# Query groups of 16 units in a ring of two, half-width projections of k and v, a transposed block by DMA, and loads moved to ScalarE

## The chip, the cores and the metric

The kernel runs on one core of one Trainium2 chip. The metric is the device time of one execution in microseconds (us). The kernel before has a median of 1043.0 us over three runs (1042.58 to 1043.64). In the text PE is TensorE (matmul), DVE VectorE, ACT ScalarE, POOL GpSimd and SP SyncE; the last three can also issue DMAs, each from a queue that it works through in order.

## The reference: two attention blocks, forward and backward

Two blocks get inputs of 2048 tokens and 448 features each, in bf16. Their outputs are concatenated, and the gradients of all eight inputs are computed for a given grad_out, so there are nine outputs.

```python
# A: linear attention, 16 heads of 28
phi = lambda t: jnp.where(t > 0, t + 1, jnp.exp(t)) + 1e-6
pq, pk = phi(q), phi(k)
kv  = jnp.einsum("bhsd,bhse->bhde", pk, v)
z   = jnp.einsum("bhsd->bhd", pk)
num = jnp.einsum("bhqd,bhde->bhqe", pq, kv)
den = jnp.einsum("bhqd,bhd->bhq", pq, z)[..., None] + 1e-6
a   = (num / den) @ wo
# B: softmax attention, 16 query heads of 28, one shared k and v head
q = x @ wq; k = x @ wk; v = x @ wv
p = softmax(einsum("bhqd,bkd->bhqk", q, k) * 28 ** -0.5)
b = einsum("bhqk,bkd->bhqd", p, v) @ wo
out   = concatenate([a, b], axis=-1)
grads = vjp(grad_out)          # of x, wqkv, wo of A; of x, wq, wk, wv, wo of B
```

## The kernel before

The kernel has four stages. Only in the third is the order of instructions written out by hand (tc.manual_schedule, line 922). In the others a planner orders the work of each engine by its estimate of when things are ready; semaphores are set by the framework.

**Phase A** (lines 124 to 546, up to about 178 us of the profile) is the whole of block A, forward and backward, in 16 tiles of 128 tokens, and the preparation of B's weights. Per-head matrices of 28x28 are kept as block-diagonal 448x448 matrices in four chunks of 128 rows: kv_blk, kvT_blk and, in the backward pass, dkvT_blk (which takes the place of kvT_blk) and dkv_blk (which lies in R4). `blkprod` (line 289) makes such a matrix by full matmuls and masks the result on DVE. dkvT_blk comes from line 450 and dkv_blk, its transpose, from line 477; dkv_blk is used at line 484. In between lie `gw` (line 430: a weight gradient, evacuated by ACT and DVE at lines 442 to 446) and the loop of line 458. All DMA transposes of phase A are issued by SP. Lines 499 to 522 prepare B's weights: wq_pad (the query weights with each head padded from 28 to 32 columns, the first of which stays free), rep (the k and v weights, each repeated four times side by side, so that a projection leaves four copies of k in the four 32-partition strips), bsel (0/1 columns that add up the squares of each head) and wo_pr (wo in 16 loads, one per head). Behind the last tile, SP transposes B's part of grad_out into R2 (line 545).

**Phase B's preparation** (lines 548 to 621) projects x. For each of four chunks of 512 tokens and for k and v there are four matmuls of 128x128x512 that accumulate; ACT (k, line 583) and DVE (v, line 580) evacuate them straight into kT_rep and vT_rep. `k_max` (line 567) finds the largest squared norm of k. Then for each chunk the queries are projected in four groups g of four heads (line 603), evacuated by ACT into R1, squared by DVE, and four matmuls with bsel add the norms up into one PSUM tile (line 609). `q_shift` (line 623) turns norms and the largest k norm into a bound on the scores, on 16 partitions; `put_shift` (line 630) writes it by DMAs into the free rows of R1, so that the score matmul subtracts it. At the end 32 narrow matmuls (line 618) turn k and v back into token rows.

**The core** (lines 647 to 1049) is the attention itself. A block b stands for 256 query tokens (qc) and two heads (a pair; g = pair // 2 is the group of four heads), and has eight units, each a step over 256 key tokens; there are 64 blocks, 512 units, and 28 more to drain the pipeline. In unit u PE makes the scores of unit u and the dP of unit w = u - 16 (`rows_SD`); ACT makes two exponentials (lines 955, 997) and one copy, cp (line 971); DVE and POOL multiply dP by the exponentials into dsT, a half each (lines 967, 972); two units later DVE transposes dsT in blocks of 32 into dsx (line 1041). Every fourth unit SP issues a DMA transpose of four units of exponentials (eN<-eT, line 999), which the dv matmuls read. Between them lie small operations once a block, among them `o_copy`, `o_norm` and `row_D`, and projections of the output in parts.

The gradient of k (`dk_m`, line 865) needs the queries transposed, in qX. For that POOL copies a group's queries of one qc, four times side by side, into a staging tile, qst, with one buffer (`qc_copy`, two copies), and SP transposes that (`qc_T`, line 860). qX holds all four groups of a qc and has two buffers, one per pool. The set for qc 0 is made ahead of unit 0, by POOL and DVE in dsT buffers; the set for the next qc in units 29, 30, 37, 38, 45, 46, 53 and 54 of the 64 that a qc takes (lines 973 to 979, 1001). So four blocks running have copies, and four have none. Block b's dk matmuls run in the odd units from 8b + 27 on.

**The end** (post_load, line 761, and lines 1051 to 1129): from unit 512 on, SP loads grad_out and x again in four and four pieces, the first of them for the gradient of wo (`gwo`); then come the remaining weight gradients and the gradient of x.

Of the kernel before, what the change touches and what calls it, by code (L numbers as in the profile page):

```python
# [9 lines left out]
ALU = mybir.AluOpType  # L10
# [15 lines left out]
def kernel(  # L26
# [49 lines left out]
    kmax2 = cst.tile([H, 1], F32, name="kmax2")  # L76
    eps = cst.tile([H, 1], F32, name="eps")
# [46 lines left out]
    def phase_A(pa, cA, cB, awk, psA):  # L124
# [95 lines left out]
        zero = [t[:, c, :] for t in (kvT_blk, kv_blk, dkv_blk) for c in range(4)]  # L220
# [49 lines left out]
        for st in range(NS):  # L270
            if st + 2 < NS:
                xT(st + 2)
            kproj(st)
            if st >= 4:
# [176 lines left out]
        prod_to(VW, wvT, dkvT_blk, True)  # L451
        with tc.issue_after(gw(gqn, 0).ins):
# [47 lines left out]
        rep = K1[1].rearrange("p c h k -> p (c h k)")[:, 0:1024].rearrange("p (w c k) -> p w c k", w=2, k=P)  # L500
        nc.gpsimd.memset(rep, 0.0)
        nc.gpsimd.memset(wq_pad, 0.0)
        for w in range(2):
            for j in range(4):
                nc.gpsimd.tensor_copy(out=rep[:, w, 0:3, 32 * j + 1:32 * j + 1 + DH], in_=wkv[:, w, 0:3, :])
                nc.gpsimd.tensor_copy(out=rep[64:128, w, 3, 32 * j + 1:32 * j + 1 + DH], in_=wkv[64:128, w, 3, :])
# [4 lines left out]
        bsel = ga[:, 4, :].rearrange("p (g k) -> p g k", k=P)  # L511
        nc.gpsimd.memset(bsel, 0.0)
        for g in range(4):
            for j in range(4):
                nc.gpsimd.memset(bsel[32 * j:32 * j + 32, g, 4 * g + j:4 * g + j + 1], 1.0)
# [5 lines left out]
        wt = flat(ga[:, 5:7, :]).rearrange("p (a k) -> p a k", k=P)  # L521
        nc.sync.dma_start_transpose(wt, rep.rearrange("p w c k -> p (w c k)"))
# [17 lines left out]
        with tc.issue_after(o1.ins):  # L540
            for w in range(2):
                nc.gpsimd.dma_start(wkvT_d[32 * w:32 * w + 32, 0:3 * P], wt[0:32, 4 * w:4 * w + 3, :])
                nc.gpsimd.dma_start(wkvT_d[32 * w:32 * w + 32, 3 * P:D], wt[0:32, 4 * w + 3, 64:128])
        for q4 in range(4):
            dma_T(v4(R2), xa, 4 * q4, 4)
        return xbT, wq_pad, rep, bsel, ga[:, 8:12, :], [flat(gaB[:, 2 * i + 8:2 * i + 10, :]).bitcast(F32) for i in range(3)]

    def phase_B_pre(pa, cA, awk, psA, io):
        xbT, wq_pad, rep, bsel, sh, tmp = io
        kT, vT, vaug, kn, qT = kT_rep, vT_rep, vaug_, kn_, R1  # L550
# [4 lines left out]
        ones16 = cA.tile([P, H], BF16, name="ones16")  # L555
        nc.gpsimd.memset(ones16[:], 1.0)
        nc.gpsimd.memset(ones16[0:1, :], 0.0)
        neg = cA.tile([P, 1], F32, name="neg")
        nc.gpsimd.memset(neg[:], 0.0)
        for j in range(4):  # L560
            nc.gpsimd.memset(neg[32 * j:32 * j + 1, :], -1.0)
        sel = cA.tile([P, 32], BF16, name="sel")
        nc.gpsimd.tensor_copy(out=sel[:], in_=identB[:, 0:32])
        nc.gpsimd.memset(sel[0:1, :], 0.0)
        kmx = cA.tile([H, NQC], F32, name="kmx")
        sqk = []
        def k_max(qc, sq):
            ps = gen([H, 512])
            mm(ps[:, :], ones16[0:32, :], sq[0:32, :])
            nc.vector.tensor_reduce(out=kmx[:, qc:qc + 1], in_=ps[:, :], axis=AX.X, op=ALU.max)  # L570

        prev = None
        for qc in range(NQC):
            for w, dst in [(0, kT), (1, vT)]:
                ps = gen([P, 512])
                for c in range(4):
                    mm(ps[:, :], rep[:, w, c, :], xbT[:, c, qc * 512:(qc + 1) * 512], start=(c == 0), stop=(c == 3))

                if w:
                    nc.vector.tensor_scalar(out=dst[:, qc * 512:(qc + 1) * 512], in0=ps[:, :], scalar1=neg[:, 0:1],  # L580
                                            scalar2=None, op0=ALU.add)
                else:
                    nc.scalar.activation(out=dst[:, qc * 512:(qc + 1) * 512], in_=ps[:, :], func=ACT.Identity,
                                         bias=neg[:, 0:1])
            sq = awk.tile([P, 512], BF16, name="osb")
            nc.vector.tensor_tensor(out=sq[0:32, :], in0=kT[0:32, qc * 512:(qc + 1) * 512],  # L586
                                    in1=kT[0:32, qc * 512:(qc + 1) * 512], op=ALU.mult)
            if prev is not None:
                k_max(qc - 1, prev)
            prev = sq  # L590
        shifts = [flat(sh)[0:H, i * 512:(i + 1) * 512] for i in range(2)] + [flat(R3)[r:r + H, 5120:5632] for r in (32, 0)]
        for qc in range(NQC):
            qs = slice(qc * 512, (qc + 1) * 512)
            pn = psA.tile([P, 512], F32, name="aacc")
# [565 lines left out]
```

## Time and profile before

| what | us |
|---|---|
| median of three runs | 1043.0 |
| the profiled execution | 1044.09 |
| its span, first to last instruction | 1042.4 |
| phase A | 0 to 178.5 |
| phase B's preparation | 178.5 to 206.5 |
| core, start (first 27 units) | 206.5 to 245.7 |
| core, in full run | 245.7 to about 970 |
| drain and end | 970 to 1042 |
| busy in the span: PE / DVE / ACT / POOL | 1003.5 / 886.9 / 865.2 / 812.3 |

Busy time is the time in which an engine had at least one compute instruction running. Matmuls overlap in PE's pipeline, so the time that one costs is read from the distance between starts, not from its own length. A row of a timeline has the start, the length, the engine, the line, the operation, the result and its inputs, the shape, the count and, in brackets, how long the engine had been idle before and which work the profile takes to have released it. Rows of "SPq" are the instants in which SP works on a DMA issue. A line can be that of a helper: most full matmuls have line 81, most tiled ones line 676.

### The profile page before, as it was taken

How to read it: one execution, taken by the hardware profiler on the slowest of the kernel's cores; microseconds unless marked ns; L12 is line 12 of the kernel's file. 1: busy time of each engine (PE TensorE's matmuls, PEld its weight loads, DVE VectorE, ACT ScalarE, POOL GpSimd, SP SyncE). 2: the span in 40 equal slices, each digit the busy share in tenths (PEclk: the TensorE clock that was granted, in tenths of full speed). 3: DMA queues.
4: the chain of work that ended last, by engine and by line, in shares of the span. 5: the costliest groups of instructions: out<-in, count | busy, mean ns of one | idle time of the engine just before them, and what ended most of it. 6: DMA issues, size and time to landing. Idle time of an engine off the chain costs nothing.

```text
span 1042.4 us, 40109 instructions
## 1 busy us (share of the span) xinstructions
PE 1003.5 (96%) x16245; PEld 485.1 (47%) x16245; DVE 886.9 (85%) x1780; ACT 865.2 (83%) x1743; POOL 812.3 (78%) x1106
## 2 busy tenths in 40 slices
PE   9999999999999999999999999999999999999998
PEld 5555554434444444444444444444444444444444
DVE  7897500669999999999999999999999999999942
ACT  6463132599999999999999999999999999999632
POOL 8601282238998998999999989998999999889860
PEclk9999999999999999999999999999999999999999
DMA  9879999299999999999999999999999999999983
GB/s 261 157 137 191 176 229 218 38 161 201 194 187 192 187 193 194 202 187 194 201 193 195 192 187 204 198 182 202 188 197 186 195 195 195 200 188 203 228 168 90
DMA packets 689058, 195.15 MB, mean 187 GB/s; under 512 B 670408, under 2 KB 686688, under 8 KB 688872
## 3 DMA queue, kind: packets, MB, share of 16 engines
q1 hardware_dynamic: 680392, 179.97, 105.0%
q0 software_dynamic: 4544, 9.46, 3.0%
q10 hardware_dynamic: 3936, 3.16, 1.0%
q8 instruction: 127, 2.08, 0.8%
q14 instruction: 59, 0.48, 0.2%
HBM read 12.60 MB, written 10.84 MB: 22 GB/s over the span
## 4 chain that ended last, share of the span: by engine, by line
PE 39%; DVE 25%; POOL 16%; ACT 8%; issue 7%; DMA 3%; DVEq 0%; SPq 0%; ACTq 0%; POOLq 0%
PE agen L81 13%; POOL dsT L972 12%; DVE dsT L967 10%; PE agen L676 9%; DVE dsx L1041 9%; PE aacc L676 8%; PE aacc L81 7%; ACT cp L971 4%; ACT eT L997 2%; DMA eN<-eT 2%; DVE doT L852 1%; DVE R L986 1%; POOL qst L856 1%; POOL prod L821 1%; PE aacc L809 1%
## 5 line engine op out<-in xcount | busy, mean ns | idle before, releaser
L972 POOL TENSOR_TENSOR dsT<-cp,eT 128x512 bf16<-128x512 bf16 x512 | 584.6, 1156 | 49.4 <-ACT cp L971 42.6
L1041 DVE STREAM_TRANSPOSE dsx<-dsT 128x512 f32<-128x512 f32 x512 | 356.7, 697 | 5.8 <-POOL dsT L972 3.2
L676 PEld LDWEIGHTS <-R 32*128 32x128 bf16 (+1 forms) x9104 | 245.1, 94 | 243.3 <-issue 192.5
L967 DVE TENSOR_TENSOR dsT<-agen,eT 128x512 bf16<-128x512 f32 x512 | 340.3, 665 | 11.3 <-PE agen L676 5.4
L971 ACT ACTIVATE cp<-agen 128x512 bf16<-128x512 f32 x512 | 327.0, 639 | 11.8 <-PE agen L676 9.7
L955 ACT ACTIVATE eT<-aacc 128x512 bf16<-128x512 f32 x512 | 325.5, 636 | 12.0 <-PE agen L676 6.8
L997 ACT ACTIVATE eT<-aacc 128x512 bf16<-128x512 f32 x512 | 333.4, 651 | 0.0
L676 PE MATMUL agen<-dsx,qX 32*32 32x512 bf16 x4024 | 264.0, 376 | 0.0
L676 PE MATMUL agen<-doT,R 32*128 32x256 bf16 x2048 | 243.5, 269 | 4.1 <-DVE dsT L967 3.2
L676 PE MATMUL aacc<-R,R 32*128 32x256 bf16 (+1 forms) x2240 | 207.9, 267 | 16.7 <-DVE doT L852 6.6
L676 PE MATMUL agen<-dsT,R 128*32 128x256 bf16 x2048 | 155.5, 273 | 0.5 <-issue 0.5
L676 PE MATMUL agen<-eT,R 128*32 128x256 bf16 x2048 | 155.5, 273 | 0.1
L676 PEld LDWEIGHTS <-qX 32*32 32x32 bf16 x4096 | 78.3, 89 | 112.5 <-issue 54.1
L676 PE MATMUL aacc<-eN,don 128*32 128x512 bf16 x1024 | 91.7, 387 | 1.0 <-DMA eN<-eT 1.0
L81 PEld LDWEIGHTS <-R 128*128 128x128 bf16 x517 | 40.9, 98 | 41.0 <-issue 10.6
L81 PE MATMUL agen<-R,R 128*128 128x448 bf16 (+1 forms) x180 | 42.1, 361 | 0.3 <-DVE pq L244 0.3
L676 PEld LDWEIGHTS <-don 128*32 128x32 bf16 x1024 | 21.1, 93 | 42.5 <-issue 42.5
L856 POOL COPY qst<-R 128x512 bf16<-128x512 bf16 x56 | 34.2, 611 | 5.0 <-DVE dsx L1041 2.5
L821 POOL TENSOR_TENSOR prod<-R,oTs 128x128 f32<-128x128 bf16 x64 | 27.5, 430 | 9.0 <-DVE oTs L817 9.0
L586 DVE TENSOR_TENSOR osb<-R 32x512 bf16<-32x512 bf16 x4 | 1.7, 413 | 35.4 <-DMA R<-xa 33.8
L427 POOL COPY pk<-R 128x256 bf16<-128x256 bf16 x4 | 1.6, 399 | 37.7 <-DVE R L389 37.7
L262 POOL TENSOR_SCALAR wdq<-wdq 128x448 bf16<-128x448 bf16 x16 | 21.1, 1326 | 12.0 <-DVE phiT L243 12.0
(235 smaller groups left out, 1000.1 us busy)
## 6 DMA issues: line engine op xcount, KB each, us to landing
eN<-eT SPq DMA_TRANSPOSE x128
xa<-in_A_x_dram SPq DMA_DIRECT2D x8, 224.0 KB
ga<-in_grad_out_dram SPq DMA_DIRECT2D x4, 448.0 KB
out_dram<-osb ACTq DMA_DIRECT2D x16, 112.0 KB
xa<-in_grad_out_dram POOLq DMA_DIRECT2D x4, 448.0 KB, 7.1
out_dram<-wdq POOLq DMA_DIRECT2D x8, 224.0 KB, 5.5
eT<-in_grad_out_dram SPq DMA_DIRECT2D x4, 448.0 KB
eT<-in_B_x_dram SPq DMA_DIRECT2D x4, 448.0 KB
```

The lines of the kernel that those rows point to most:

```text
L81: nc.tensor.matmul(out_ap, lhsT=lhsT, rhs=rhs, start=start, stop=stop, tile_position=(0, 0))
L262: nc.gpsimd.tensor_scalar(out=wq_n[:, st, 0:D], in0=wq_n[:, st, 0:D], scalar1=1.0, scalar2=None, op0=ALU.min)
L676: nc.tensor.matmul(out, lhsT=lhsT, rhs=rhs, start=start, stop=stop, tile_position=pos, skip_group_check=True)
L809: nc.tensor.transpose(onp[:, qb, :, :].rearrange("p h c -> p (h c)"), oTs[0:64, qb * P:(qb + 1) * P], identF[0:64, 0:64], tile_position=(0 ...
L821: nc.gpsimd.tensor_tensor(out=prod[b][:], in0=dnv, in1=os_, op=ALU.mult)
L856: eng.tensor_copy(out=st.rearrange("p (b s) a j -> p b s a j", s=2)[:, :, s, :, :], in_=src.unsqueeze(2).to_broadcast([P, 4, 4, 32]))
L955: nc.scalar.activation(out=eT(u)[:, 0, :], in_=sp[0][:, :], func=ACT.Exp, scale=scale)
L967: nc.vector.tensor_tensor(out=dst[:, 0, :], in0=dp[0][:, :], in1=ew[:, 0, :], op=ALU.mult)
L971: nc.scalar.activation(out=cp[:, :], in_=dp[1][:, :], func=ACT.Copy)
L972: nc.gpsimd.tensor_tensor(out=dst[:, 1, :], in0=cp[:, :], in1=ew[:, 1, :], op=ALU.mult)
L997: nc.scalar.activation(out=eT(u)[:, 1, :], in_=sp[1][:, :], func=ACT.Exp, scale=scale)
L1041: nc.vector.transpose(out=dsx[b][:, tp, :, :, :].rearrange("p h t c -> p (h t c)").bitcast(F32), in_=dsT[y][:, :, :].rearrange("p h c -> p ...
```

## The change

- **dkv_blk** is no longer computed; four DMA transposes from dkvT_blk, issued by ScalarE right behind line 451, fill it, and POOL clears 64 rows. Four zero fills of it by ACT (line 275) go.
- **wo_pr** is loaded by four DMAs in place of 16. rep holds the weights once (32 columns of k and 32 of v), bsel has 32 columns, and their copies, fills, transposes and stores shrink with them.
- **Projection of k and v**: two PSUM tiles in place of eight, each with two chunks of tokens one above the other (64 partitions each); the two halves are matmuls with 64 columns of weights, issued in turn into the two halves of PE's columns. Four DMAs by POOL and four by SP replicate k and v into the strips of kT_rep and vT_rep. k_max, the token rows and the squares work on 64-partition halves, and the first two of these stand between the second and third query group of chunk 0.
- **Norms**: four matmuls into the four 32-column strips of PE, one per group, behind the first query group of the next chunk (the last ones at the end); q_shift works on 128 partitions.
- **Core**: qX has one group (qc, g), G = 4 qc + g, and a ring of two buffers from one pool. Group G is copied by POOL in units 16G + 13 and 16G + 14 and transposed by SP in unit 16G + 14, G = 0 too; nothing is made ahead of unit 0. Pools of 12 KiB a partition less follow from it, and later pools move up. row_D of block 0, which was skipped, runs in unit 12.
- **Behind the core** the four loads of grad_out are issued by ScalarE.

```diff
+        for c in range(4):
+            r = DC_ROWS[c]
+            nc.scalar.dma_start_transpose(dkv_blk[:, :, c * P:c * P + r], blks[0:r, (12 + c) * D:(12 + c) * D + 512])
+        nc.gpsimd.memset(dkv_blk[64:128, 3, :], 0.0)
...
-        for h in range(H):
-            g, j = divmod(h, 4)
-            nc.sync.dma_start(wo_pr[32 * j + 1:32 * j + 1 + DH, g, 0:D], B_wo[h * DH:(h + 1) * DH, :])
+        for j in range(4):
+            nc.sync.dma_start(wo_pr[32 * j + 1:32 * j + 1 + DH, :, 0:D],
+                              B_wo.rearrange("(g j r) d -> j r g d", j=4, r=DH)[j, :, :, :])
...
-        blkprod(dkv_blk, [lambda c, i: cols(GT[0], c, i), lambda c, i: cols(GT[1], c, i)], [lambda c: woT[:, c, :]])
...
+        for p in range(2):
+            ps = gen([P, 512])
+            for c in range(4):
+                for a in range(2):
+                    i_ = nc.tensor.matmul(ps[64 * a:64 * a + 64, :], lhsT=rep[:, c, 0:64],
+                                          rhs=xbT[:, c, (2 * p + a) * 512:(2 * p + a + 1) * 512], start=(c == 0),
+                                          stop=(c == 3), tile_position=(0, 64 * a), skip_group_check=True)
...
+        for w, dst in [(0, kT_rep), (1, vT_rep)]:
+            for a in range(2):
+                for j in range(4):
+                    [nc.gpsimd, nc.sync][w].dma_start(
+                        dst[32 * j:32 * j + 32, :].rearrange("r (p a s) -> r p a s", p=2, a=2)[:, :, a, :],
+                        kvs[64 * a + 32 * w:64 * a + 32 * w + 32, :, :])
...
+        def norms(qc):
+            pn = psA.tile([P, 512], F32, name="aacc")
+            for g in range(4):
+                i_ = nc.tensor.matmul(pn[32 * g:32 * g + 32, :], lhsT=bsel[:, 0:32], rhs=sqs[:, 4 * (qc % 2) + g, :], start=True,
+                                      stop=True, tile_position=(0, 32 * g), skip_group_check=True)
...
+                if qc == 0 and g == 1:
+                    k_max(0)
+                    k_max(1)
+                    kv_nat(0)
+                    kv_nat(1)
+                if qc and g == 0:
+                    pn = norms(qc - 1)
...
-                nc.sync.dma_start(t[:, :, 0:D], go2[rows, D:2 * D].rearrange("(t p) d -> p t d", p=P))
+                nc.scalar.dma_start(t[:, :, 0:D], go2[rows, D:2 * D].rearrange("(t p) d -> p t d", p=P))
...
+        def qc_T(G):
+            qX[G] = pq_.tile([P, 4, 2, P], BF16, name="qX")
+            nc.sync.dma_start_transpose(qX[G].rearrange("p b s c -> p (b s) c"), qst.rearrange("p n a j -> p (n a j)"))
...
-                if 0 <= gq < 4 and u < 448:
-                    if gq == 0 and iq == 0:
-                        qX[qq] = (pqb_ if qq % 2 else pqa_).tile([P, 4, 2, 512], BF16, name="qX")
-                    if iq < 2:
-                        qc_copy(nc.gpsimd, qst, qq, gq, iq)
+                if u == 12:
+                    row_D(0)
+                if hasS and u % 16 in (13, 14):
+                    qc_copy(u // 16, u % 16 - 13)
...
-                    if 0 <= gq < 4 and iq == 1 and u < 448:
-                        qc_T(qst, qq, gq)
+                    if u % 16 == 14:
+                        qc_T(u // 16)
```

More of the change, by code (lines that the diff above doesn't have):

```diff
@@ L219, in phase_A @@
             nc.gpsimd.memset(t[64:128, 3, :], 0.0)
-        zero = [t[:, c, :] for t in (kvT_blk, kv_blk, dkv_blk) for c in range(4)]
+        zero = [t[:, c, :] for t in (kvT_blk, kv_blk) for c in range(4)]
         wvT = w_T(wvT_, w3, 2 * D)
@@ L563, in phase_B_pre @@
[L563 to L572, printed above, removed]
+            nc.gpsimd.memset(sel[32 * j:32 * j + 1, :], 0.0)
+        kmx = cA.tile([P, NQC], F32, name="kmx")
@@ L573, in phase_B_pre @@
         for qc in range(NQC):
-            for w, dst in [(0, kT), (1, vT)]:
+            qs = slice(qc * 512, (qc + 1) * 512)
+            for g in range(4):
                 ps = gen([P, 512])
                 for c in range(4):
[L577 to L584, printed above, removed]
@@ L615, in phase_B_pre @@
[L615 to L619 removed]
+                    mm(ps[:, :], wq_pad[:, c, g * P:(g + 1) * P], xbT[:, c, qs], start=(c == 0), stop=(c == 3))
+                nc.scalar.activation(out=qT[:, g, qs], in_=ps[:, :], func=ACT.Copy)
+                nc.vector.tensor_tensor(out=sqs[:, 4 * (qc % 2) + g, :], in0=qT[:, g, qs], in1=qT[:, g, qs], op=ALU.mult)
```

149 lines of the change are left out of this document (67 added, 82 removed).

## Prediction

> **What bounds the kernel now.** The profile's stretches come first, because the change touches several stages with different limits.
>
> ```profile
> 178.50:206.50 28.00, 27.71 (x150) 11.83 (x147) 16.02 (x36) 14.43 (x24) 7.25 (x13) 1.00 0.33 61
> 206.50:245.70 39.20, 35.21 (x399) 14.47 (x395) 28.78 (x55) 34.79 (x68) 19.54 (x28) 1.00 0.97 167
> 245.70:970.00 724.30, 701.07 (x13860) 332.18 (x13860) 705.73 (x1389) 717.32 (x1454) 674.36 (x858) 1.00 1.21 194
> 970.00:1042.00 72.00, 64.86 (x694) 30.56 (x694) 36.16 (x66) 25.01 (x48) 36.62 (x52) 1.00 0.74 159
> ```
>
> Columns: length, then busy time of PE, weight loads, DVE, ACT and POOL, granted clock (1.00 throughout), DMA share, GB/s. From 178.5 to 206.5 (B's projections) PE is busy 27.7 of 28.0 us and every other engine at most 16: work taken from PE there shortens the stage. In the core (245.7 to 970) ACT is busy 99%, DVE 97%, PE 97%, POOL 93%.
>
> Next, the core in blocks of eight units, cut at DVE's evacuation of line 986 (once a block). Most blocks last 11.78 us (the last nine 12.08); a few are longer, such as the fourth and fifth of these:
>
> ```profile
> 434.96 0.43 DVE L986 TENSOR_SCALAR R<-agen 64x256 bf16<-64x256 f32 x1
> 446.74 0.43 DVE L986 TENSOR_SCALAR R<-agen 64x256 bf16<-64x256 f32 x1
> 458.52 0.43 DVE L986 TENSOR_SCALAR R<-agen 64x256 bf16<-64x256 f32 x1
> 470.76 0.43 DVE L986 TENSOR_SCALAR R<-agen 64x256 bf16<-64x256 f32 x1
> 483.81 0.43 DVE L986 TENSOR_SCALAR R<-agen 64x256 bf16<-64x256 f32 x1
> ```
>
> The last two steps are 12.24 and 13.05 us. Over blocks 12 to 52 the excess over 11.78 adds up to 7.8 us. Most of it stands at the end of the bursts in which four blocks running copy queries for the transpose (blocks 19, 20, 34, 35, 40, 48, 51). POOL's and SP's timelines say why:
>
> ```profile
> 464.57 0.61 POOL L856 COPY qst<-R 128x512 bf16<-128x512 bf16 x1 [0.46 <-DMA qX<-qst]
> 477.62 0.61 POOL L856 COPY qst<-R 128x512 bf16<-128x512 bf16 x1 [1.32 <-DVE dsx L1041]
> ...
> 460.19 1.30 SPq L860 DMA_TRANSPOSE qX<-qst  x1
> 461.60 11.66 SPq L999 DMA_TRANSPOSE eN<-eT  x2
> 473.35 1.26 SPq L860 DMA_TRANSPOSE qX<-qst  x1
> 474.72 10.65 SPq L999 DMA_TRANSPOSE eN<-eT  x2
> ```
>
> The staging tile qst has one buffer. Its transpose waits behind the big ones in SP's queue, about 6 us after the copies (454.0 to 460.2; 467.4 to 473.4), and POOL is released 4.3 us after the issue (460.19 to 464.57, 473.35 to 477.62; I read the second release as this DMA too, since the DVE work named has no part in qst). So the next block's first copy, due 11.78 - 1.66 (the step between the two copies) = 10.1 us after this block's second, comes too early. SP itself is over its time in such a block: 10.7 + 1.3 + gaps = 12.1 us against 11.78.
>
> **The change part by part.**
>
> (1) *Core: one query group per 16 units.* A staging reuse now has 23.56 - 1.66 = 21.9 us where it needs 10.4: these waits go. SP's demand in 16 units is 4 x 5.4 + 1.4 = 23.0 of 23.56 us, POOL's about 11.7 (with copies: 459.07 to 471.25 between two operations of line 821, less the wait of 0.46) + 10.6 (the same less two copies at 0.57) + 0.65 for a store = 22.9. What remains of the 7.8 us is about 0.3 at each of three output transposes (line 1048), and about 0.9 of the stalls around 805 to 818 us, where PE waited for eN: 6.0 us go (bounds 2.5 and 7.5). Eight more copies (64 for 56, 0.61 us each) fall mostly where none were; the last groups lie in blocks of 12.08 us, where POOL needs the same 22.9 of 24.2. The ring: group G is filled from unit 16G+14 on, its buffer was last read at 16G+9, and it is first read at 16G+27. Ready after 6 + 4.3 us, or 7 units: 6 units to spare.
>
> (2) *B's projections, PE.* Start to start from its timeline:
>
> ```profile
> 182.09 0.38 PE L81 MATMUL agen<-osb,ones 32*16 32x512 bf16 x1
> 182.41 1.90 PE L81 MATMUL agen<-pk,K 128*128 128x512 bf16 x8
> 184.24 0.38 PE L81 MATMUL agen<-osb,ones 32*16 32x512 bf16 x1
> ...
> 110.65 1.70 PE L85 MATMUL aacc<-R,xa 128*64 128x448 bf16 x16
> ...
> 429.76 0.40 PE L676 MATMUL aacc<-eN,don 128*32 128x512 bf16 x4
> ```
>
> Removed: 32 k/v matmuls at 1.83/8 = 0.229, 7.3; four k_max at 0.32, 1.3; 16 norm matmuls at 0.22, 3.5; 32 narrow ones at 0.033 (27 in 0.88), 1.05: together 13.1 us. Added: 16 half-width matmuls. The line 85 row has such pairs, two halves of the columns side by side: 16 start within 1.63 us at 448 columns, so 0.116 at 512, 1.9 us. Norms in four column strips: four of 512 columns take 0.40 alone and eight 0.62, so 0.3 a chunk, 1.2 us. k_max with half the rows: 0.7 (0.5 if pairs overlap, 1.3 if not). 16 matmuls of 64 columns: 0.7 (0.5 to 1.0). Two waits are new. At the end nothing lies between the last query projection and its norms (before, the narrow matmuls did): ACT 0.60, DVE 0.43 and handovers, 1.2 us. And DVE gets four maxima (0.61) and four copies (about 0.35), 3.9 us, in one place, against 3.1 us of PE work that needs no buffer from it: 0.7 (0 to 1.5). Added 6.4, gain 6.7 us. If no pairs overlapped, k/v would cost 3.7 and norms 3.5, and the gain fall to 2.6; at best it is 8.5. ACT loses three evacuations of 0.69 and DVE three of 0.73; both have room.
>
> The Trainium skill's TensorEngine Tiling (Array Packing), Restrictions, says that column tiling goes without fast weight loading. By that alone a pair might cost what two full matmuls do, and the sum would be that of rival D; the line 85 row, where 16 of them keep their 0.10 us pace with their loads, disagrees for this shape.
>
> (3) *dkv_blk by transpose.* 32 matmuls (126.29 to 128.14) go, 1.85 us on a PE without idle time there. Added are four issues on ScalarE. SP's like ones take 1.4 each (two in 2.79); on ScalarE that is 5.6 us. If they go out when dkvT_blk is masked (about 102), they end before its next work at 110.4 and land long before 126. Gain 1.85; nothing below that in the good case, the bad one is rival B.
>
> (4) *Replication of k and v by eight DMAs.* POOL's four issues (0.55 each) follow its last at 182.3, and land near 188; the first unit would start near 197. SP's four follow the transposes that end at 185.5; v is first used at unit 16. Hidden; each us later than 197 would cost one.
>
> (5) *Fewer loads, copies and fills in set-up* (wo_pr, rep, bsel, wkvT_d): POOL's chain there ends at 146.4 and only stores and a load follow that is needed at 171; SP has the slack. Nothing. Four zero fills less on ACT, which waits for PE there: nothing.
>
> (6) *Start of the core.* Four POOL and four DVE copies and four SP transposes go; PE runs without a gap there but for 0.70 at 207.7, where it waits for ACT. I take 0.4 (0 to 0.7). The added row_D of block 0 (DVE 0.28, POOL 0.4) falls into 6.8 us of POOL idleness.
>
> (7) *Loads behind the core by ScalarE.* PE waits 0.16 us for the first at 982.6, so little is to be won. ScalarE's issue at unit 516 must wait for POOL's product of unit 515, and behind it stands ScalarE's cp, for which POOL and PE wait; cp already waits for POOL there (1.32 and 0.80 us at 977.9 and 979.2). Cost between -0.2 and 1.3; I take 0, the nearer end.
>
> Sum: 6.0 + 6.7 + 1.85 + 0.4 = 15.0 us. The profiled execution took 1044.1 (span 1042.4 and 1.7 around it), so 1029.1 by its time; it lay 1.1 above the median, 1043.0. Forecast **1028.0**, its own range 1024 to 1032.
>
> **Rivals.**
>
> *B: ScalarE's transposes queue behind SP's.* SP has transposes at 105.0 to 111.6 and on to 117.7; ScalarE is in order, and its evacuations at 110.4 and 112.4 stand behind. If it starts after 111.6 + 4.3 and issues 5.6 us, the one at 112.4 is 9 us late; DVE's next products wait for that, and PE has four buffers of 0.76 = 3 us of cover: 6 lost. If the planner lets the evacuations by and the transposes wait for 117.7, dkv_blk lands at 117.7 + 4.3 + 5.6 + 4.3 = 132 for a use at 126: the same 6. Both at once reach 12. Time 1034 (1031 to 1040). For it: SP's queue is full there. Against: the rows show idle ScalarE from 103.5 to 110.4. Chance 0.14. The Trainium skill's DMA: Bandwidth & Descriptors, section Silent corruption: two transposing streams in flight at once, demands just this wait of the later stream. By it this rival is the rule; no run here shows it, since all transposes before go out from SP.
>
> *C: the core keeps its stalls*, since line 999 and 1048 alone make them; gain 9: 1034. For: the stall at 805 us. Against: the releases of qst above. 0.10.
>
> *D: pairs don't overlap* on these shapes, so the change doesn't do what it should: 4.1 less, 1032. 0.06.
>
> *E, slower: the query groups come late.* Before, a whole set had over 30 units of lead; now 6. If SP ran more than 19 - 4.3 = 14.8 us behind (it runs 5 to 6.5 behind), PE would wait for each group; at the longest stall seen, 1.3 us, 32 groups cost 41: 1069. At 0.5 us a group it would be level. 0.08.
>
> **How the numbers follow.** Forecast 0.62. B, C and D end at 1032 to 1034. All that is faster: 0.88. Within 0.2% (2.1 us, about what a measurement of this kernel can tell from no change): B's worst together with C, or E at its threshold, 0.04. Slower: 0.08. The range 1024 to 1036 holds the forecast, most of B, C and D, and the bounds of the waits.
>
> **What would show it.** Right: the stage of B's projections 20 to 22 us long, 16 half-width matmuls starting within 2 us; blocks of 11.8 us throughout, no POOL wait ahead of qst; no matmuls for dkv_blk. Wrong: idle PE in the stages of lines 458 or 484, DVE or ACT waiting there for ScalarE's queue; PE waits for qX in the core; a gap longer than 2 us ahead of unit 0.

## The result and the profile after

The changed kernel takes 1049.7 us (median of four runs, 1049.1 to 1051.8); the kernel before took 1042.9 beside it (1042.6 to 1043.6). The ratio is 1.007, with a 95% interval of 1.005 to 1.0091: it is **slower by 6.8 us** where the forecast was 15 us faster. The profiled execution has a span of 1047.7 us (before 1042.4). The stages of that execution, with the columns of the prediction's first view (the second number is PE's busy time, the one ahead of the last two the granted clock):

```profile
178.50:189.00 10.50, 10.50 (x58) 5.29 (x58) 0.00 (x0) 2.72 (x5) 1.45 (x2) 1.00 1.02 212
189.00:209.80 20.80, 20.66 (x119) 8.04 (x121) 14.12 (x34) 13.09 (x21) 11.37 (x22) 1.00 0.80 117
209.80:249.00 39.20, 34.25 (x384) 14.34 (x389) 25.50 (x51) 34.91 (x68) 17.43 (x25) 1.00 0.86 160
249.00:970.10 721.10, 700.57 (x13860) 332.50 (x13860) 704.85 (x1388) 715.94 (x1454) 677.65 (x862) 1.00 1.20 194
970.10:1047.70 77.60, 67.09 (x694) 30.75 (x694) 36.30 (x66) 25.04 (x48) 37.60 (x54) 0.96 0.80 164
```

B's projections start at 189.0 instead of 178.5 and take 20.8 us instead of 28.0. The core is cut again at DVE's evacuation once a block (line 986, now 995); b0 is its first row, b61 the 62nd. The ledger of the two executions:

| stage | before | after | difference | forecast |
|---|---|---|---|---|
| phase A, to the start of B's projections | 178.5 | 189.0 | +10.5 | -1.85 |
| B's projections | 28.0 | 20.8 | -7.2 | -6.7 |
| start of the core, to b0 | 39.2 | 39.2 | 0 | -0.4 |
| b0 to b53 | 632.8 | 627.3 | -5.5 | -6.0, with the next |
| b53 to b61 | 96.9 | 99.2 | +2.3 | |
| b61 to the end | 67.0 | 72.2 | +5.2 | 0 |

**Phase A.** Three engines' timelines of the changed kernel, ACT, SP and PE in this order:

```profile
97.84 1.83 ACT L249 ACTIVATE gaT<-aacc 128x448 bf16<-128x448 f32 x4 [0.42 <-PE aacc L81]
111.46 10.76 ACTq L454 DMA_TRANSPOSE R<-blks  x4
122.26 0.95 ACT L326 CAST KOT<-agen 128x448 bf16<-128x448 f32 x2 [22.59 <-DMA R<-blks]
...
105.58 10.31 SPq L419 DMA_TRANSPOSE ga<-gaT  x2
123.48 2.48 SPq L109 DMA_TRANSPOSE ga<-R  x2
...
122.84 14.02 PE L81 MATMUL agen<-KOT,R 128*128 128x448 bf16 x62 [9.96 <-ACT KOT L326]
```

ACT's first transpose goes out only at 111.46, and its four take until 122.22, because SP's take turns with them: SP too stands still for ScalarE's to land, twice (its waits: total us, times, longest):

```profile
SPq L109 <- DMA R<-blks: 7.4, 1, 7.4
SPq L419 <- DMA R<-blks: 4.7, 1, 4.7
```

The evacuation of line 326 stands behind them in ACT's queue, and PE idles 9.96 us for it. PE's clock falls meanwhile (the last but two column):

```profile
110.00:115.00 5.00, 2.89 (x23) 1.23 (x21) 0.00 (x0) 0.00 (x0) 0.00 (x0) 1.00 0.34 73
115.00:120.00 5.00, 0.00 (x0) 0.00 (x0) 0.00 (x0) 0.00 (x0) 0.00 (x0) 0.69 0.65 122
120.00:125.00 5.00, 2.16 (x6) 0.74 (x6) 0.00 (x0) 2.72 (x6) 1.44 (x3) 0.50 0.32 63
125.00:130.00 5.00, 5.00 (x22) 2.38 (x21) 4.89 (x9) 0.08 (x1) 3.85 (x6) 0.79 0.96 205
```

so that the 62 matmuls take 14.0 us, where 64 take 12.3 in kernels below that have no gap there. The gap (9.96) and these 2 us, less the 1.85 of the product, are 10.1 of the 10.5 us.

**B's projections** in PE's timeline:

```profile
188.96 1.92 PE L572 MATMUL agen<-pk,K 128*64 128x512 bf16 x16
192.65 0.61 PE L593 MATMUL aacc<-pq,ga 64*128 64x512 bf16 x4
193.09 0.53 PE L601 MATMUL agen<-ga 64*128 64x64 bf16 x16
201.03 0.73 PE L610 MATMUL aacc<-pq,ga 128*32 128x512 bf16 x4
```

The 16 half-width matmuls of k and v take 1.9 us, as forecast; the norms take 0.66 a chunk (start of one to start of the next) and not 0.3: three of the four start together at 201.03, and the last at 201.38, when DVE has squared its input (line 625). The maxima and token rows take 0.44 and 0.46, forecast 0.7 each.

**Core and end.** SP's timeline of the changed kernel, in mid-core and at the end of it, and that of ACT for the last exponential:

```profile
449.62 22.15 SPq L1008 DMA_TRANSPOSE eN<-eT  x4
471.86 1.26 SPq L879 DMA_TRANSPOSE qX<-qst  x1
473.22 21.58 SPq L1008 DMA_TRANSPOSE eN<-eT  x4
...
954.56 22.99 SPq L1008 DMA_TRANSPOSE eN<-eT  x4
977.64 1.92 SPq L879 DMA_TRANSPOSE qX<-qst  x1
979.66 7.53 SPq L1008 DMA_TRANSPOSE eN<-eT  x1
...
969.56 0.60 ACT L1006 ACTIVATE eT<-aacc 128x512 bf16<-128x512 f32 x1
```

and the same end before the change:

```profile
971.00 5.91 SPq L999 DMA_TRANSPOSE eN<-eT  x1
...
969.45 0.61 ACT L997 ACTIVATE eT<-aacc 128x512 bf16<-128x512 f32 x1
```

Four eN transposes and one query group take SP from 449.62 to 473.22, 23.6 us; two blocks take 23.56. Between 260 and 960 us SP has no gap over 0.7 us. The last eN transpose, whose data are ready at 970.16, goes out 9.5 us later; before, 1.0 us later. The table gives this distance for some of the 128 eN transposes (start of the issue less the end of the exponential that completes its four units):

| SP behind, us, at transpose | 8 | 32 | 64 | 96 | 112 | 127 |
|---|---|---|---|---|---|---|
| before | 4.6 | 9.1 | 8.9 | 10.8 | 9.4 | 1.0 |
| after | 2.6 | 4.0 | 5.9 | 8.4 | 11.0 | 9.5 |
| after, no late transposes | 3.2 | 6.3 | 8.6 | 8.1 | 9.9 | 1.6 |
| product, four groups ahead, loads by SP | 4.4 | 6.3 | 8.4 | 10.9 | 8.7 | 0.0 |
| the same, seven groups fewer | 4.3 | 2.6 | 3.8 | 3.8 | 3.4 | 0.0 |
| the same, each group twice | 6.8 | 14.3 | 14.7 | 13.7 | 11.2 | 2.3 |

Transpose 112 is the first of the last 64 units. There the kernel before makes no groups any more and SP catches up; the changed one makes four more.

### The profile page after: what moved, and what is told of

The parts are those of the page before. It is cut to its first block, busy times and chain, and to the rows that moved or that the text cites. A ratio compares the mean times of both kernels' runs of the same rounds, so it can differ in the third digit from the quotient of the medians.

```text
span 1047.7 us, 39942 instructions
## 1 busy us (share of the span) xinstructions
PE 998.0 (95%) x16173; PEld 480.2 (46%) x16181; DVE 880.5 (84%) x1770; ACT 861.0 (82%) x1736; POOL 816.5 (78%) x1102
## 4 chain that ended last, share of the span: by engine, by line
PE 41%; DVE 32%; ACT 9%; DMA 7%; issue 6%; POOL 4%; ACTq 0%; DVEq 0%; SPq 0%
DVE dsT L979 13%; PE agen L81 12%; DVE dsx L1050 11%; PE agen L693 11%; PE aacc L693 9%; PE aacc L81 5%; DMA eN<-eT 5%; ACT cp L983 4%; ACT eT L1006 3%; POOL dsT L984 2%; DVE R L995 2%; PE aacc L826 2%; DVE doT L869 2%; DVE Dq L852 1%; DMA ga<-gaT 1%
## 5 line engine op out<-in xcount | busy, mean ns | idle before, releaser
L984 POOL TENSOR_TENSOR dsT<-cp,eT 128x512 bf16<-128x512 bf16 x512 | 585.9, 1158 | 45.4 <-ACT cp L983 35.6
L693 PE MATMUL agen<-doT,R 32*128 32x256 bf16 x2048 | 246.1, 269 | 6.2 <-ACT cp L983 3.3
L693 PE MATMUL aacc<-R,R 32*128 32x256 bf16 (+1 forms) x2240 | 207.0, 267 | 13.7 <-DVE doT L869 5.6
L874 POOL COPY qst<-R 128x512 bf16<-128x512 bf16 x64 | 39.2, 613 | 5.0 <-DMA R<-dsT 5.0
L262 POOL TENSOR_SCALAR wdq<-wdq 128x448 bf16<-128x448 bf16 x16 | 21.1, 1328 | 12.3 <-DVE phiT L243 12.2
```

Of the source, the lines that this page charges most:

```text
L262: nc.gpsimd.tensor_scalar(out=wq_n[:, st, 0:D], in0=wq_n[:, st, 0:D], scalar1=1.0, scalar2=None, op0=ALU.min)
L693: nc.tensor.matmul(out, lhsT=lhsT, rhs=rhs, start=start, stop=stop, tile_position=pos, skip_group_check=True)
L874: nc.gpsimd.tensor_copy(out=qst.rearrange("p (b s) a j -> p b s a j", s=2)[:, :, s, :, :], in_=src.unsqueeze(2).to_broadcast([P, 4, 4, 32]))
L984: nc.gpsimd.tensor_tensor(out=dst[:, 1, :], in0=cp[:, :], in1=ew[:, 1, :], op=ALU.mult)
```

## The experiments

Ratios are to the kernel before on the same chip (its medians there: 1041.7 to 1042.8), with the 95% interval.

### dkv_blk by transposes

The kernel before with this part alone:

```diff
+            nc.scalar.dma_start_transpose(dkv_blk[:, :, c * P:c * P + r], blks[0:r, (12 + c) * D:(12 + c) * D + 512])
...
-        blkprod(dkv_blk, [lambda c, i: cols(GT[0], c, i), lambda c, i: cols(GT[1], c, i)], [lambda c: woT[:, c, :]])
```

> The kernel before, with the transposes of dkv_blk by ScalarE in place of its product, alone. If they cost what the stage ahead of B shows in the changed kernel: about 10 us more than before, 1050 to 1055. If the loss comes from their lying together with the other edits: 1041 to 1046.

Measured: 1051.9 us, 1.0084 (1.0067 to 1.0101): **9.1 us slower**. B's projections start at 189.6, with the same 9.9 us of idle PE ahead of line 326's products. So the loss is this part's own.

The changed kernel with the product back:

```diff
-            nc.scalar.dma_start_transpose(dkv_blk[:, :, c * P:c * P + r], blks[0:r, (12 + c) * D:(12 + c) * D + 512])
+        blkprod(dkv_blk, [lambda c, i: cols(GT[0], c, i), lambda c, i: cols(GT[1], c, i)], [lambda c: woT[:, c, :]])
```

> The changed kernel with the product for dkv_blk (and its masking and zeros) put back as before, without the four transposes. By the ledger of the two profiles the stage ahead of B's projections then costs what it did before (10.5 us less than now): 1039, and 1038 to 1041. Against the run with SyncE's transposes this gives the price of product against transposes: by the prediction the transposes are worth 1.85 us, so that this kernel would be about 2 us above that one; if the transposes hold SyncE's later ones up, it is below it.

Measured: 1043.3 us, 1.0009 (0.999 to 1.0028). B's projections start at 179.2, near the 178.5 of before. The total is 4 us over the expectation: in its profiled execution b0 to b53 takes 631.3, and the tail 72.8.

Neither product nor transposes, only the zero fills of before:

```diff
-            nc.scalar.dma_start_transpose(dkv_blk[:, :, c * P:c * P + r], blks[0:r, (12 + c) * D:(12 + c) * D + 512])
...
-        zero = [t[:, c, :] for t in (kvT_blk, kv_blk) for c in range(4)]
+        zero = [t[:, c, :] for t in (kvT_blk, kv_blk, dkv_blk) for c in range(4)]
```

> The changed kernel, leaving dkv_blk at zero: neither its product nor its transposes are done. The floor of this step: B's projections start 1.85 us earlier than with the product (179.3), so near 177.5 us, against 189 with the transposes; the rest as with the product alone: 1040 to 1043 us. If it starts no earlier than the product's kernel, the forecast gain of 1.85 us was never there.

Measured: 1039.2 us, 0.9974 (0.996 to 0.9987). B's projections start at 177.7, 1.6 us ahead of the kernel with the product. So 1.6 of the 1.85 us of PE work that the forecast took out were there to be had; the transposes cost more.

The same transposes, ordered on ACT behind its evacuations:

```diff
+                    lastA[0] = nc.scalar.activation(out=odd, in_=al[3][64:128, :], func=ACT.Copy)
...
+        with tc.issue_after(lastA[0].ins):
+            for c in range(4):
+                r = DC_ROWS[c]
+                nc.scalar.dma_start_transpose(dkv_blk[:, :, c * P:c * P + r], blks[0:r, (12 + c) * D:(12 + c) * D + 512])
```

> The changed kernel with the four transposes still issued by ScalarE, but behind the evictions of the first gradient product (L326, L446 and L442 come before them in ScalarE's order). If the loss is that ScalarE's evictions stand behind the transposes in its order: 1037 to 1041, as with SyncE. If it is the alternation of two queues itself (SyncE's transposes wait for ScalarE's to land): still 1045 to 1050, since the same eight or so transposes take turns, only later.

Measured: 1052.3 us, 1.0084 (1.0051 to 1.0118), in runs from 1041.3 to 1058.4. Line 326's gap is gone, but B's projections still start at 186.9. SP and PE in its timeline:

```profile
140.69 27.59 SPq L98 DMA_TRANSPOSE gaT<-wdq  x4
...
113.04 12.28 PE L81 MATMUL agen<-KOT,R 128*128 128x448 bf16 x64
168.79 1.67 PE L81 MATMUL agen<-ga,gaT 128*128 128x448 bf16 x4 [6.38 <-DMA gaT<-wdq]
```

PE now waits for SP's transposes of gaT, which go out 9 us later than in the kernel with the product (shown below). The blocking of ACT's queue was only the first place where the loss showed.

And by SP:

```diff
-            nc.scalar.dma_start_transpose(dkv_blk[:, :, c * P:c * P + r], blks[0:r, (12 + c) * D:(12 + c) * D + 512])
+            nc.sync.dma_start_transpose(dkv_blk[:, :, c * P:c * P + r], blks[0:r, (12 + c) * D:(12 + c) * D + 512])
```

> The changed kernel, with the four transposes of dkv_blk issued by SyncE instead of ScalarE; nothing else. Theory (ScalarE stands still 22.6 us because its four transposes take turns with SyncE's, each waiting for the other queue's last one to land, and everything ScalarE has to evict, L326 first, is queued behind them; TensorE then idles about 10 us and comes back at half clock): ScalarE's gap ahead of L326 goes, and B's projections start near 178 instead of 189 us in the profile, so 1037 to 1041 us. Rival 1 (TensorE waits there for the products' operands, transposed gradients among them, whoever issues): no change, 1048 to 1051. Rival 2 (the four transposes only move their queueing to SyncE, whose later transposes of B's x then come late): about half of it, 1043 to 1046.

Measured: 1062.1 us, 1.0151 (1.0086 to 1.0217): the slowest of these, though one of its four runs took 1048.1, so that the size is uncertain; both the theory and rival 2's half of the loss are off. SP and PE in its timeline:

```profile
143.18 35.64 SPq L98 DMA_TRANSPOSE gaT<-wdq  x4
...
150.50 1.67 PE L81 MATMUL agen<-ga,gaT 128*128 128x448 bf16 x4 [5.23 <-DMA gaT<-wdq]
175.18 1.68 PE L81 MATMUL agen<-ga,gaT 128*128 128x448 bf16 x4 [13.46 <-DMA gaT<-wdq]
```

In the changed kernel with the product, SP's same row:

```profile
131.34 13.78 SPq L98 DMA_TRANSPOSE gaT<-wdq  x4
```

The loads that POOL issues there (from 146.0 with the transposes by SP), in the view of the DMA issues; the last number is the time to their landing, by SP and then with the product:

```profile
xa<-in_grad_out_dram POOLq DMA_DIRECT2D x4, 448.0 KB, 20.7
```

```profile
xa<-in_grad_out_dram POOLq DMA_DIRECT2D x4, 448.0 KB, 9.4
```

With the product the gaT transposes go out from 131.3 and are over when the four loads come. Twelve us later they run beside them, and both take more than twice as long. So SP's transposes are a chain that phase A hangs on; four more of them, from whichever queue, move all later ones.

Not all of the twelve us are the four transposes' own time (5.5 us in SP's queue). The edit also has POOL clear 64 rows of dkv_blk, and POOL waits for their landing in every variant with transposes (22.2 us in the changed kernel). In the run by SP the fill of wo_pr (line 475) stands behind that in POOL's queue, and SP waits for the fill:

```profile
POOL R L455 <- DMA R<-blks: 22.3, 1, 22.3
SPq L477 <- POOL R L475: 5.3, 1, 5.3
```

No run separates this clear from the transposes, so its share of the loss is open.

### The loads behind the core

The changed kernel with the loads by SP again:

```diff
-                nc.scalar.dma_start(t[:, :, 0:D], go2[rows, D:2 * D].rearrange("(t p) d -> p t d", p=P))
+                nc.sync.dma_start(t[:, :, 0:D], go2[rows, D:2 * D].rearrange("(t p) d -> p t d", p=P))
```

> The changed kernel with the four loads behind the core issued by SyncE again. Theory (ScalarE's fourth load waits for the landing of the transpose that used its completion counter before it, that of group 126, and cp at unit 519 is queued behind the load): the tail after block 61 falls from 72.2 to about 67 us, so 1044 to 1046 us. Rival (the transposes come out of the core late and hold cp's readers and the tail by themselves): 1048 to 1051, with the wait for eN then on another engine.

Measured: 1052.1 us, 1.0095 (1.0065 to 1.0126): no gain, so my theory of the tail fell, and the wait is on PE now. SP and PE:

```profile
977.73 4.95 SPq L1008 DMA_TRANSPOSE eN<-eT  x1
982.79 1.20 SPq L792 DMA_DIRECT2D eT<-in_grad_out_dram  x2
...
987.63 1.65 PE L81 MATMUL aacc<-eT,R 128*128 128x448 bf16 x4 [5.32 <-DMA eT<-in_grad_out_dram]
```

The loads now stand behind a late SP. Its lateness is the cause, as the runs on the groups show.

The kernel before with its loads by ScalarE, alone:

```diff
-                nc.sync.dma_start(t[:, :, 0:D], go2[rows, D:2 * D].rearrange("(t p) d -> p t d", p=P))
+                nc.scalar.dma_start(t[:, :, 0:D], go2[rows, D:2 * D].rearrange("(t p) d -> p t d", p=P))
```

> The kernel before, with the four loads behind the core issued by ScalarE, alone. If they collide with the last eN transpose (in the runs with ScalarE's loads its issue takes 6.5 to 11.2 us, with SyncE's 4.9 to 5.9): 2 to 5 us slower than before, 1044 to 1047. If the collision needs a SyncE that is late: within 1.5 us of before.

Measured: 1045.6 us, 1.0033 (1.002 to 1.0047): **3.3 us slower**, where SP was in time. The profiled execution is the fastest of its twelve (1041.6): its b0 to b53 happens to take 627.1, but its tail 69.8, 2.8 more than before the change. Its chain of waits has the last eN transpose, and SP's timeline the last two, like this:

```profile
965.87 19.27 DMA eN<-eT
```

```profile
960.81 14.31 SPq L999 DMA_TRANSPOSE eN<-eT  x2
```

The transpose issued at 965.87 takes 19.3 us to land, beside loads issued from 964.8 on; those that stand in the chains of the kernel before take 8.4 and 9.1. With the loads by SP, behind it, the last two are issued in 11.4 us and none stands in the chain (the kernel with four groups ahead):

```profile
958.66 11.44 SPq L1011 DMA_TRANSPOSE eN<-eT  x2
970.21 1.07 SPq L789 DMA_DIRECT2D eT<-in_grad_out_dram  x2
```

### The query groups

The changed kernel without the transposes of the last four groups:

```diff
-                    if u % 16 == 14:
+                    if u % 16 == 14 and u < 448:
                         qc_T(u // 16)
+                    elif u % 16 == 14:
+                        qX[u // 16] = qX[u // 16 - 2]
```

> The changed kernel, leaving out the transposes of the last four query groups (units 462, 478, 494 and 510); dk of the last eight blocks is computed from the buffers' old content. GpSimd's copies for these groups stay. If SyncE's transposes are the price of the late groups: as the run with early groups, b53 to b61 at 97 us and the tail at 67, so 1041 to 1044 us. If GpSimd's copies are (some 1.5 us each beside a GpSimd that is busy 22.9 of 24.2 us in two blocks): b53 to b61 stays near 99 us and the tail near 72, 1047 to 1050.

Measured: 1045.5 us, 1.0028 (1.0008 to 1.0047), in runs from 1042.5 to 1050.8: some 4 us less than the changed kernel; in the profiled execution (1042.7) b53 to b61 takes 97.6 and the rest 67.5. SP's transposes are the price, and not POOL's copies, which are all still there.

All groups made by unit 446, with six buffers:

```diff
+        early = {8 * (7 * G // 4) + 13: G for G in range(32)}
...
-                    if u % 16 == 14:
-                        qc_T(u // 16)
+                    if u - 1 in early:
+                        qc_T(early[u - 1])
```

> The changed kernel with six instead of two transposed-query buffers, and the 32 groups made in units 13 to 446 (on average one per 14 units) instead of one per 16 units to the end; nothing else. Theory (in units 448 to 511 each group's transpose lies between SyncE's eN transposes, which have no room left there: blocks are late at b53 to b61, the queue comes out of the core some 5 us late, and the tail pays it, whoever issues the loads): b53 to b61 falls from 99.2 to about 97 us and b61 to the end from 72.2 to about 67, so 1041 to 1044 us. Rival (the loads by ScalarE hold the tail by themselves): the core gains 2 us, the tail stays above 71, 1047 to 1049.

Measured: 1053.5 us, 1.0095 (1.0074 to 1.0117). b53 to b61 falls to 96.7, as expected, but b0 to b53 rises to 634.2: the same work is now paid earlier. The tail stays at 71.3, with ScalarE's loads beside the last transpose (it lands after 19.4 us). The same ring with the product for dkv_blk (both edits):

> The changed kernel with the product for dkv_blk put back and the early query groups: both supposed losses gone, the gains in B's projections (7.2 us) and in the core's bursts (5.5 us) kept. By the ledger 1042.9 - 7.2 - 5.5 = 1030, and 1029 to 1034. If only one of the two losses is understood: 1036 to 1043.

Measured: 1046.7 us, 1.0036 (1.0021 to 1.0051): far from the 1030 of the ledger. b0 to b53 takes 639.9. From here on I took SP's work inside the core as one sum. The product, with four groups ahead of the core as before the change:

```diff
+            for G in range(4):
+                st = qst if G == 3 else pd_.tile([P, 2, 512], BF16, name="dsT").rearrange(
+                    "p a (n j) -> p a n j", j=32).rearrange("p a (n b) j -> p (a n) b j", b=4)
+                qc_copy(G, 0, st)
+                qc_copy(G, 1, st, nc.vector)
+                qc_T(G, st)
...
-                    if u % 16 == 14:
-                        qc_T(u // 16)
+                    if u % 16 == 14 and u < 448:
+                        qc_T(u // 16 + 4)
```

> The changed kernel with the product for dkv_blk put back; the first four query groups transposed ahead of the core (as before the change, from the dsT buffers and qst) and group G from 4 on in unit 16(G-4)+13, so that none falls after unit 446; six buffers. SyncE then has as many transposes inside the core as before the change, evenly spread. Theory (SyncE's transposes fill the core; each group beyond the 28 that fit is paid at the end): B's projections start near 179, b0 lies near 240 to 242, b0 to b53 takes 627 to 630, b53 to b61 97 and the end 67 us, so 1031 to 1036. Rival (after the earlier start the core meets other stalls, as the run with the product and early groups did at 640 for b0 to b53): 1040 to 1046.

Measured: 1040.3 us, 0.9969 (0.9952 to 0.9986), in runs from 1032.9 to 1042.9. In the profiled one b53 to b61 takes 96.6 and the end 66.9, as expected, but b0 to b53 632.8: what it was before the change. With the loads by SP (the first edit of the part on the loads):

> The kernel with the product and four groups ahead, with the four loads behind the core issued by SyncE again. If SyncE is on time at the end of the core, the issuer of the loads is worth nothing: within 1.5 us of that kernel. If ScalarE's loads are worth a SyncE time of 2.3 us (four issues at 0.54 to 0.6 us) in the tail: 2 us slower than it. If they hold ScalarE: faster than it by 1 to 3 us.

Measured: **1035.7 us, 0.9934 (0.9922 to 0.9947)**, runs from 1035.1 to 1036.8; 4.6 us below the last one, in line with the 3.3 us of the loads alone. b0 to b53 is 632.3. The product without the last four groups' transposes (the edits of two runs above together):

> The changed kernel with the product for dkv_blk put back, leaving out the transposes of the last four query groups (dk of the last eight blocks comes from old content). By the two runs that took one of these away each: 9.7 us less ahead of the core and some 6 us less behind b53, so 1032 to 1035 us. If the earlier start of the core is lost again inside it (the run with the product alone lost 4 us there): 1036 to 1041.

Measured: 1038.1 us, 0.9959 (0.9947 to 0.9971), the second case: b0 to b53 takes 631.0, and ScalarE's loads again make the last eN transpose land late (18.8 us).

So an even ring gave nothing between b0 and b53 here. Two runs on the kernel of 1035.7 us tell whether SP sets this. With seven groups fewer:

```diff
-                    if u % 16 == 14 and u < 448:
+                    if u % 16 == 14 and u < 448 and u // 16 % 4 == 3:
+                        qX[u // 16 + 4] = qX[u // 16 + 3]
+                    elif u % 16 == 14 and u < 448:
                         qc_T(u // 16 + 4)
```

> The kernel with the product, four groups ahead and the loads by SyncE, leaving out the transposes of seven of the 28 groups inside the core (every fourth; dk of their blocks comes from another group's queries). GpSimd's copies stay. Theory (SyncE's transposes fill the core: four eN transposes at 5.55 us and one group at 1.36 make 23.56 us, which is two blocks of 11.78): SyncE gains 9.5 us of room, never falls 10 us behind, the stall at b47 (15.6 instead of 11.8 us) and the small ones go, b0 to b53 falls from 632.3 to 626 or 627: 1029 to 1032 us. Rival (GpSimd or the stores at b47 make these stalls): 1034 to 1037, as with all groups.

Measured: 1032.6 us, 0.991 (0.9896 to 0.9925). b0 to b53 takes 627.0. DVE's rows of blocks 47 and 48, with all groups and then with fewer:

```profile
798.08 0.43 DVE L998 TENSOR_SCALAR R<-agen 64x256 bf16<-64x256 f32 x1
813.71 0.43 DVE L998 TENSOR_SCALAR R<-agen 64x256 bf16<-64x256 f32 x1
```

```profile
796.73 0.43 DVE L998 TENSOR_SCALAR R<-agen 64x256 bf16<-64x256 f32 x1
808.51 0.43 DVE L998 TENSOR_SCALAR R<-agen 64x256 bf16<-64x256 f32 x1
```

A block of 15.6 us has become one of 11.8, with every POOL copy and store in place. The whole gains 3.1 us for the 9.5 us that SP no longer works. With all groups again, and each one's transpose twice:

```diff
                         qc_T(u // 16 + 4)
+                        two = pq_.tile([P, 4, 2, P], BF16, name="qX2", bufs=1)
+                        nc.sync.dma_start_transpose(two.rearrange("p b s c -> p (b s) c"), qst.rearrange("p n a j -> p (n a j)"))
```

> The same kernel with all groups, but each of the 28 inside the core transposed twice, the second time into a buffer that nothing reads; nothing is left out and GpSimd does no more. Theory (SyncE full): 28 times 1.36 us is 38 us more work for a queue with 10 us or less of room, so 25 to 38 us longer: 1060 to 1075 us, with TensorE waiting for eN in most of the core. Rival (SyncE has room inside the core): under 1045.

Measured: 1075.8 us, 1.0323 (1.0309 to 1.0336): **40 us slower** than the kernel of 1035.7, for 28 transposes of 1.38 us, 38.6. PE's waits for eN, with all groups once and then twice (total us, times, longest):

```profile
PE aacc L690 <- DMA eN<-eT: 2.5, 2, 2.2
```

```profile
PE aacc L690 <- DMA eN<-eT: 31.4, 23, 3.5
```

The work added to SP in the core is paid in full here. Finally B's projections, with the smaller set-up, alone: the product, the loads by SP, and the groups in the old bursts.

```diff
-                    if u % 16 == 14 and u < 448:
-                        qc_T(u // 16 + 4)
+                    if 0 <= gq < 4 and iq == 1 and u < 448:
+                        qc_T(qst, qq, gq)
```

> The kernel with the product and the loads by SyncE, with the query groups in bursts as before the change: only B's projections and the set-up around them are left of the change. If SyncE's sum sets the core and spreading is worth nothing: the same as the kernel with four groups ahead, 1035 to 1037 us. If the bursts cost what the forecast gave them (6 us, at least 2.5): 1038 to 1042.

Measured: 1035.5 us, 0.9939 (0.9927 to 0.9951): the same as with the even ring (1035.7). In its profile POOL waits for the staging tile in the core again, and PE less for eN:

```profile
POOL qst L871 <- DMA qX<-qst: 3.9, 5, 1.8
PE aacc L691 <- DMA eN<-eT: 2.0, 3, 1.1
```

With the ring, POOL's wait in the core is gone and PE's is 2.5. **Spreading the groups is worth nothing in this kernel; B's projections and the set-up around them are worth 6.8 us.**

## Why the prediction was wrong

**Step (3) failed: "Gain 1.85; nothing below that in the good case, the bad one is rival B."** The transposes cost 9.1 us alone. The forecast's good case was ACT issuing "when dkvT_blk is masked (about 102)"; they went out from 111.46 on. This is rival B, given 0.14 and a price of 6 ("Both at once reach 12"); phase A came out 12.35 us above its forecast. Its mechanism was right and my refusal of it was not: I argued from an idle ScalarE, while the queue that mattered was SP's. The Trainium skill's DMA: Bandwidth & Descriptors, Silent corruption: two transposing streams in flight at once, demands that the later stream wait; the trace agrees, with the two queues' six transposes taking turns between 105.6 and 122.2. What the rival lacked is what the runs by SP and behind the evacuations show: even with the evacuations free, B's chain of transposes starts later and then collides with the loads. In the changed kernel itself it doesn't come to that collision (gaT's transposes end at 154.1, the loads start at 157.7); there the gap and the clock are the loss. That POOL's queue is blocked by the clear, too, was not foreseen.

**Step (1) failed in its sum for SP: "4 x 5.4 + 1.4 = 23.0 of 23.56 us".** Start to start an eN transpose takes 5.55 us before and 5.59 after (medians of 88), so the sum is 4 x 5.55 + 1.36 = 23.56, all of the time there is. The 0.15 us I missed on each is the whole room of the step. With no room, taking the wait away from qst gains nothing: the kernel of 1035.7 has no such wait in the core, PE waits 2.5 us for eN in place of 2.0, and the time is the same. Rival E's "it runs 5 to 6.5 behind" was too small as well: at the table's transposes up to 112 the kernel before is 4.6 to 10.8 behind. "The last groups lie in blocks of 12.08 us, where POOL needs the same 22.9 of 24.2" asked the wrong engine: with SP's lag no longer worked off in the last 64 units, four more transposes came out of the core with it, 6.3 us in the profiled executions (99.2 + 72.2 less 97.6 + 67.5) and some 4 in the medians. And step (6) counted the four transposes ahead of the core as something to be rid of (0.4 us, measured 0), while they were SP's cheapest four.

The 5.5 us that the profile after shows between b0 and b53 is not shown to be the ring's gain. One execution of the kernel before with old bursts has 627.1 there (the run with ScalarE's loads), another 632.8; other kernels with bursts have 631.3 and 634.4, and kernels with an even ring 626.7 to 632.8. Leaving out the runs with fewer groups and with each twice: where it is near 627, SP is 7.6 to 8.7 us behind at transpose 96; where it is 631 or more, 9.2 to 11.5. What decides between the two was not found. With an even ring, the six kernels without the product have 626.7 to 627.4 and the four with it 631.0 to 632.8; but the one with bursts and 627.1 has the product, so its presence alone does not decide.

**Step (7) failed: "I take 0".** The loads alone cost 3.3 us, outside the bounds of -0.2 to 1.3. The bounds priced ScalarE's wait for POOL; what the profile's chain shows is the last eN transpose, landing late beside the loads.

**Step (2) was right**: 6.7 forecast, 7.2 in the profile, 6.8 in the kernel with this part and the set-up alone. The sum is closer than its terms: the norms cost 1.4 us more than forecast, the maxima and token rows 0.5 less, and the two new waits, forecast at 1.9, are left with about 0.6. Pairs of half-width matmuls overlap, which clears rival D. **Steps (4) and (5)** cost nothing that a profile shows. Rival E named the slower case with groups that come late; the groups came in time, and it was eN that did not.

Part by part, alone: +9.1 (dkv_blk), +3.3 (loads), -6.8 (projections), which is +5.6 of the +6.8 measured; the rest, 1.2, is left for the ring with its late groups and for what the parts do to each other. They do not simply add: in the changed kernel giving the loads back to SP gains nothing, and leaving out the four late transposes gains some 4 us.

## What to carry to other kernels

Add up each DMA queue like an engine, in start-to-start times over the stage: a queue whose sum equals the stage had no cover for anything here, wherever in the stage it was put, while the four transposes ahead of the stage cost nothing that the ledger shows. A wait that disappears beside a full queue need not shorten anything. Before a transfer is given to a second queue, ask what is in flight beside it: here a transpose beside plain loads took two to three times as long. The part worth keeping was the one that took work off the engine that bounds its stage; with the set-up, alone, it makes 1035.5 us.

## What was not expected of the hardware

- The transposes' length goes by bytes: an eN transpose moves 1 MiB (128 x 4096 two-byte values) in 5.55 us, a query group 256 KiB in 1.36: 189 and 193 GB/s. The Trainium skill's DMA: Bandwidth & Descriptors, section Latency and other measured facts, gives 261 GB/s for a transpose with a non-contiguous middle dimension and 350 to 400 for a contiguous one; the measurement is lower, and it decides. Whether SP's queue or the DMA engines behind it (a share of 1.20 in the core's row) set this rate was not separated.
- Transposes and plain loads slow each other: 13.8 against 35.6 us for four transposes of gaT (27.6 in the run behind the evacuations), 9.4 against 20.7 us for the landing of four loads, 19 against 8 to 10 us for the landing of an eN transpose.
- In some 10 us of idle PE its clock fell to 0.50, and it was full again only between 125 and 130 us: by the mean of 0.79 in that slice at about 127, 4 us after work resumed at 122.8. The price is 2 us on 62 matmuls. The Trainium skill's TensorE: Matmul & The Clock Gate, Part 1: The HAM clock gate, has half the clock after an idle window of about 3.4 us; the rows agree (0.69 in the slice from 115, 0.50 in the next).
